# Attention plus mixture-of-experts on one core: another order of loads, copies and sums at the start of the attention part

## The chip, the cores and the metric

The kernel runs on one core of a Trainium2 chip. The metric is the device time of one execution in microseconds (us), lower is better. The core has five engines with their own instruction streams: TensorE (PE: matmuls and transposes; PEld: its weight loads), VectorE (DVE), ScalarE (ACT), GpSimd (POOL) and SyncE (SP), which here only issues transfers. Sixteen DMA engines move the data.

## The reference, cut to what matters

Four batches of eight heads, 768 tokens and 64 channels go through a local attention with block summaries, and the result goes through a top-1 mixture of eight experts. Per batch and head:

```python
block, window = 32, 16
k_sum = k.reshape(B, H, nb, block, D).max(axis=3)      # summary keys: maximum of 32 keys
v_sum = v.reshape(B, H, nb, block, D).mean(axis=3)     # summary values: mean of 32 values
scores_l = where(|i - j| < 16, scale * q @ k.T, -1e9)  # local part
scores_s = scale * q @ k_sum.T + log(block)            # 24 summaries
a = softmax(concat([scores_l, scores_s]))
attn = a @ concat([v, v_sum])
# x = attn as 3072 rows of 512; per row one expert e of 8:
out = gate * sigmoid(x @ w_output_gate)[e] * (relu(x @ w1[e]) @ w2[e])
```

The inputs q, k, v are 6.3 MB each in float32.

## The kernel before, in words

**Attention** works in 48 stages, `stages = [(b, tok, g)]`: batch `b` (4), tile of 128 tokens `tok` (6), half of the heads `g` (2). A pair of tiles is a step `u = tok // 2`; within a step the stages count `s = 0..3`. A stage `i` runs `scores(i)` (PE, line 338, into `sp`; then four masks with a minimum on DVE, line 346, and four exponentials on ACT, line 348), `turn_p(i)` (PE transposes, line 356, and an evacuation `pT` on ACT or DVE) and `values(i)` (PE, line 367, and the division on DVE, lines 375 to 377). In the loop `scores(i+1)` comes ahead of `turn_p(i)` and `values(i-1)`.

**Keys and queries** come in pieces of 256 tokens (`load`, line 209, 512 KB each, into `raw`). `reorder` (line 220 on DVE, 218 on ACT) copies a piece into `nat` so that two heads stand side by side. `prep_k` transposes it on PE (line 289, `ktr`), evacuates it into `kt` on ACT (line 201) and takes the maxima `km` on DVE (line 303); `k_sum` writes these into `kt` (line 312). `prep_q` does the same for queries (`qtr`, `qt`). The string `RE` says which engine reorders which piece: the first three are the key pieces of batch 0, then the query pieces 0 and 1 of batch 0, all later queries, all later keys.

**Values** are needed twice. `load_vw` (lines 271 and 272) loads for each block of 64 tokens a window of 64 + 32 rows into one of nine tiles `vw`. `load_vm` (line 228, 768 KB, four heads) loads the values for the means into `vm`; `v_sum` adds up 32 rows: on DVE for the first half of the heads of batch 0 (line 239), on POOL by halving additions for all others (lines 250 and 254). `mean` scales (line 260 or 262) and writes the 24 means of each head to the DRAM tensor `vs_dr` (line 263), and `load_vsum` (line 278) reads them back into each `vw` tile, behind the 64 + 32 rows. So a stage's `values` needs the means, by way of DRAM.

**What sets the order.** All loads of q, k, v, `vw`, means and weights are issued by SP, in the order of the program: a load whose source or buffer isn't ready holds up all loads behind it. The other engines' instructions are put in order ahead of time by a list scheduler that works with estimated durations and takes the program's order as priority; on the chip each engine then keeps that order. `tc.add_manual_dep(..., NoSync, SCHED_ONLY)` ties an instruction behind another in that order and adds no wait. Ahead of the attention, `route_setup` runs `WARM` = 44 matmuls of 128x128 bf16 on PE (line 161) whose result is not used, and POOL clears the nine `vw` tiles (line 191) and sets a column of ones in each (line 192).

The order of the program at the start is: key pieces 0, 1, 2, query piece 0, `vm` 0 and 1; reorder and prepare the keys, the queries; `k_sum`; `vw` of tile 0, query piece 1, `vw` of tile 1; the sums of values; reorder query piece 1; key piece 0 of batch 1; `vw` of tile 2; the means into tiles 0, 1, 2; `vm` 0 of batch 1; then the stages. In a stage with `g == 0` the loop reorders the next keys and queries ahead of `scores(i+1)`.

**The experts** start inside the last batch (`late_work`: lists, rows and weights of the first expert slot) and fill the time from about 190 us to the end, with PE in the lines 845 to 847 and 943 to 945.

Of the kernel before, what the change touches and what calls it, by code (L numbers as in the profile page):

```python
# [25 lines left out]
W = 120  # L26
# [8 lines left out]
VR = 9  # L35
VP = 72
ON_DVE = ("p1", "lt", "ls")
RE = "vavavvv"
SPLIT = 1
TAT = 0  # L40
XAT = 6
ROUTE_AT = (-1, 0, 1, 2, 4)
WARM = 44
SCALE = 1.0 / math.sqrt(D)
N, DM, E, F = B * S, H * D, 8, 1024
NT = N // P
# [131 lines left out]
def attention(tc, const, sa, sb, st, ps, dr, q, k, v, id_sb, c_sb, wg_sb, x_dr, l_dr, rt, late_work):  # L178
# [9 lines left out]
        KT.append(t)  # L188
    for i in range(VR):
        t = sb.tile([W, H, VP], F32, name=f"vw{i}", tag=f"vw{i}", bufs=1)  # L190
        nc.gpsimd.memset(t, 0.0)
        nc.gpsimd.memset(t[:, :, D:D + 1], 1.0)
        VW.append(t)
    def evac(what, dst, src, scale=None):
# [16 lines left out]
            src[b, :, 256 * u:256 * (u + 1), :].rearrange("h (p j) d -> p h (j d)", j=2))  # L211
        raws[kind, b, u] = raw

    def reorder(kind, b, u, engine="v"):
        t = (sa if kind == "k" else sb).tile([P, 2, H, D], F32, name=f"nat_{kind}{b}{u}", tag=f"nat{kind}", bufs=BUFS["nat" + kind])
        r = raws.pop((kind, b, u)).rearrange("p h j d -> p j h d")
        if engine == "a":
            nc.scalar.activation(t, r, AF.Copy)
        else:
            {"v": nc.vector, "p": nc.gpsimd}[engine].tensor_copy(t, r)  # L220
        nat[kind, b, u] = t

    vm = {}
# [9 lines left out]
    def v_sum(b, o, half):  # L233
        t = vm[b, o]
        if (b, o) == (0, 0):
            if half == 0:
                vs[b, o] = sb.tile([96, D], F32, name=f"vs{b}{o}", tag="vs", bufs=2)
            hs = slice(32 * half, 32 * half + 32)
            i = nc.vector.tensor_reduce(out=vs[b, o][:, hs], in_=t.rearrange("p (s d) -> p d s", d=D)[:, hs, :], axis=AX.X,
                                        op=ALU.add)  # L240

            tc.add_manual_dep(i.ins, km["last"].name, mybir.DependencyInfo(mybir.DependencyClass.NoSync,
                                                                           mybir.DependencyReason.SCHED_ONLY))
            if half == 1:
                mean(b, o, vs[b, o])
            return

        n = 16 * D
        if half == 0:
            nc.gpsimd.tensor_tensor(t[:, 0:n], t[:, 0:n], t[:, n:2 * n], ALU.add)  # L250
# [78 lines left out]
    def scores(i):  # L329
        b, tok, g = stages[i]  # L330
        u, tt = tok // 2, tok % 2
        qt, kt = QT[(3 * b + u) % 2], KT[b % 2]
        sp = ps.tile([P, 4, P], F32, name=f"sp{b}{tok}{g}", tag="S", bufs=PB["S"])
        for x in range(2):
            for y in range(2):
                li = 2 * tt + y
                blk = 4 * u + li
                nc.tensor.matmul(sp[:, 2 * x + y, 0:W], lhsT=qt[:, 2 * g + x, li, :],  # L338
                                 rhs=kt[:, 2 * g + x, blk * KW:blk * KW + W], start=True, stop=True)
        sm = sb.tile([P, 4, W], F32, name=f"sm{b}{tok}{g}", tag="sm", bufs=BUFS["sm"])  # L340
        mn = sb.tile([P, 4], F32, name=f"mn{b}{tok}{g}", tag="mn", bufs=BUFS["mn"])
        pr = sb.tile([P, 4, W], F32, name=f"pr{b}{tok}{g}", tag="pr", bufs=BUFS["pr"])
        for c in range(4):
            blk = 2 * tok + (c % 2)
            m = C_MASK + W * (1 if blk == 0 else (2 if blk == NB - 1 else 0))
            nc.vector.tensor_tensor_reduce(out=sm[:, c, :], in0=sp[:, c, 0:W], in1=c_sb[:, m:m + W], scale=1.0,  # L346
                                           scalar=3.0e38, op0=ALU.add, op1=ALU.min, accum_out=mn[:, c:c + 1])
# [173 lines left out]
    for i, (b, tok, g) in enumerate(stages):  # L521
# [31 lines left out]
        if b == B - 1:  # L553
# [1 line left out]
            take = w[:-(-len(w) // 2)] if g == 0 else w[:]  # L555
            del w[:len(take)]
            second += take
        if i + 1 < n:
            scores(i + 1)
        for work in first[:1]:  # L560
            work()
        turn_p(i)
        second = first[1:] + second
        for work in second:
            work()
        if i > 0:
            values(i - 1)
            pb, ptok, pg = stages[i - 1]
# [488 lines left out]
```

## Time and profile before

| what | value |
|---|---|
| time, median of 3 runs | 540.3 us (539.38 to 544.87) |
| profiled execution, own time | 537.39 us |
| its span in the trace | 535.6 us |
| PE busy | 492.9 us, 92% of the span |
| DVE / ACT / POOL busy | 387.0 / 336.2 / 204.1 us |
| granted TensorE clock, mean | 0.978 |
| moved by the DMA engines | 117.98 MB, mean 220 GB/s |

Times inside the profile count from the start of the span. A row of the timeline gives start, duration, engine, line, operation, output and input, how many instructions are merged in the row, and in brackets the idle time of the engine before it and what ended it. A row of the windows gives for a stretch of time the busy us of each engine with the number of instructions, the granted TensorE clock as a share of full speed (PEclk), the mean busy share of the DMA engines and what they moved. SPq rows are transfers being issued by SP, not the transfers.

### The profile page before, as it was taken

How to read it: one execution, taken by the hardware profiler on the slowest of the kernel's cores; microseconds unless marked ns; L12 is line 12 of the kernel's file. 1: busy time of each engine (PE TensorE's matmuls, PEld its weight loads, DVE VectorE, ACT ScalarE, POOL GpSimd, SP SyncE). 2: the span in 40 equal slices, each digit the busy share in tenths (PEclk: the TensorE clock that was granted, in tenths of full speed). 3: DMA queues.
4: the chain of work that ended last, by engine and by line, in shares of the span. 5: the costliest groups of instructions: out<-in, count | busy, mean ns of one | idle time of the engine just before them, and what ended most of it. 6: DMA issues, size and time to landing. Idle time of an engine off the chain costs nothing.

```text
span 535.6 us, 12274 instructions
## 1 busy us (share of the span) xinstructions
PE 492.9 (92%) x3880; PEld 428.5 (80%) x3880; DVE 387.0 (72%) x1238; ACT 336.2 (63%) x753; POOL 204.1 (38%) x231
## 2 busy tenths in 40 slices
PE   5899998789987999999999999999999999999990
PEld 5687887587766798789898998989897887987870
DVE  8877888479958868987666667675667767768660
ACT  4776786487769756554655656565567567558460
POOL 7527157245443432333735071421333421611321
PEclk9789999899999999999999999999999999999996
DMA  8989999899698577595966749486476796696640
GB/s 246 242 207 249 231 247 207 178 222 263 157 196 226 167 236 253 190 193 183 331 205 218 230 166 319 143 284 214 183 264 204 258 304 237 216 311 241 198 159 30
DMA packets 117052, 117.98 MB, mean 220 GB/s; under 512 B 53787, under 2 KB 78651, under 8 KB 116192
## 3 DMA queue, kind: packets, MB, share of 16 engines
q1 hardware_dynamic: 107584, 97.02, 64.5%
q0 software_dynamic: 9376, 19.91, 11.3%
q8 instruction: 36, 0.59, 0.5%
q14 instruction: 56, 0.46, 0.3%
HBM read 106.30 MB, written 13.79 MB: 224 GB/s over the span
## 4 chain that ended last, share of the span: by engine, by line
PE 61%; DMA 17%; DVE 6%; SPq 5%; issue 4%; ACT 3%; POOL 0%; POOLq 0%; ACTq 0%; DVEq 0%
PE hp L846 8%; PE hp L845 8%; PE hp L847 8%; PE yp L945 7%; PE yp L943 7%; PE yp L944 7%; DMA xg<-x_dr,lst_w 5%; PE sp L338 4%; DMA raw_q<-in_q_dram 4%; DMA vw<-vs_dr 3%; PE pv L367 3%; DMA raw_k<-in_k_dram 2%; PE pt L356 2%; PE xp L827 2%; SPq L272 1%
## 5 line engine op out<-in xcount | busy, mean ns | idle before, releaser
L845 PE MATMUL hp<-xhl,w1h 128*128 128x256 f32 x384 | 108.4, 284 | 1.1 <-ACT w2h L815 1.1
L846 PE MATMUL hp<-xhl,w1h 128*128 128x256 f32 x384 | 108.8, 284 | 0.0
L847 PE MATMUL hp<-xhl,w1l 128*128 128x256 f32 x384 | 108.5, 283 | 0.1
L943 PE MATMUL yp<-w2h,hh 128*128 128x512 f32 x216 | 86.5, 401 | 0.3 <-ACT hh L914 0.2
L945 PE MATMUL yp<-w2h,hl 128*128 128x512 f32 x216 | 84.9, 395 | 0.1
L944 PE MATMUL yp<-w2l,hh 128*128 128x512 f32 x216 | 84.9, 393 | 0.0
L794 POOL DMA_INDIRECT xg<-x_dr,lst_w x26 | 30.5, 1173 | 123.5 <-PE xp L827 118.7
L845 PEld LDWEIGHTS hp<-xhl,w1h 128*128 128x128 f32 x384 | 73.2, 191 | 2.9 <-issue 1.5
L846 PEld LDWEIGHTS hp<-xhl,w1h 128*128 128x128 f32 x384 | 73.5, 191 | 2.1 <-DVE xhl L830 0.9
L847 PEld LDWEIGHTS hp<-xhl,w1l 128*128 128x128 f32 x384 | 73.5, 191 | 0.3 <-issue 0.3
L348 ACT ACTIVATE pr<-sm,mn 128x120 f32<-128x120 f32 x192 | 61.5, 386 | 18.3 <-DVE mn L346 17.9
L848 ACT ACTIVATE hh<-hp 128x256 fp32r<-128x256 f32 x96 | 35.2, 380 | 53.4 <-PE hp L847 43.6
L849 DVE SCALAR_TENSOR_TENSOR hl<-hp,hh 128x256 fp32r<-128x256 f32 x96 | 38.8, 419 | 37.6 <-ACT hh L848 22.9
L338 PE MATMUL sp<-kt,qt 128*128 128x120 f32 x384 | 53.6, 287 | 2.2 <-DVE mn L346 0.8
L338 PEld LDWEIGHTS sp<-kt,qt 128*128 128x128 f32 x384 | 48.4, 199 | 5.6 <-issue 2.3
L945 PEld LDWEIGHTS yp<-w2h,hl 128*128 128x128 f32 x216 | 40.4, 188 | 9.8 <-DVE hl L915 1.2
L346 DVE CUSTOM_DVE_ANT_0 sm<-sp,c_sb 128x120 f32<-128x120 f32 x192 | 42.2, 276 | 8.2 <-PE sp L338 5.3
L943 PEld LDWEIGHTS yp<-w2h,hh 128*128 128x128 f32 x216 | 40.7, 188 | 8.6 <-ACT hh L914 0.7
L944 PEld LDWEIGHTS yp<-w2l,hh 128*128 128x128 f32 x216 | 40.7, 188 | 7.9
L356 PE MATMUL pt<-id_sb,pr 128*120 128x128 f32 x192 | 38.7, 288 | 4.6 <-ACT pr L348 1.9
L367 PE MATMUL pv<-vw,pT 120*64 120x65 f32 x768 | 36.3, 231 | 6.8 <-DVE xs L377 2.8
L367 PEld LDWEIGHTS pv<-vw,pT 120*64 120x64 f32 x768 | 28.6, 139 | 16.0 <-issue 7.9
(736 smaller groups left out, 1039.5 us busy)
## 6 DMA issues: line engine op xcount, KB each, us to landing
vw<-in_v_dram SPq DMA_DIRECT2D x88, 96.0 KB
raw_k<-in_k_dram SPq DMA_DIRECT2D x12, 512.0 KB
raw_q<-in_q_dram SPq DMA_DIRECT2D x12, 512.0 KB
vm<-in_v_dram SPq DMA_DIRECT2D x8, 768.0 KB
x_dr<-xs POOLq DMA_DIRECT2D x24, 256.0 KB
vw<-vs_dr SPq DMA_DIRECT2D x36, 48.0 KB
vw<-in_v_dram SPq DMA_DIRECT2D x8, 64.0 KB
xg<-x_dr,lst_w POOLq DMA_INDIRECT x26
```

The lines of the kernel that those rows point to most:

```text
L338: nc.tensor.matmul(sp[:, 2 * x + y, 0:W], lhsT=qt[:, 2 * g + x, li, :], rhs=kt[:, 2 * g + x, blk * KW:blk * KW + W], start=True, stop=True)
L346: nc.vector.tensor_tensor_reduce(out=sm[:, c, :], in0=sp[:, c, 0:W], in1=c_sb[:, m:m + W], scale=1.0, scalar=3.0e38, op0=ALU.add, op1=ALU. ...
L348: nc.scalar.activation(pr[:, c, :], sm[:, c, :], AF.Exp, bias=mn[:, c:c + 1], scale=-1.0)
L356: nc.tensor.transpose(pt[:, c, :], pr[:, c, :], id_sb)
L367: nc.tensor.matmul(po[64 * y:64 * y + 64, 2 * x + hh, :], lhsT=pT[:, 2 * x + y, 64 * hh:64 * hh + 64], rhs=VW[(NB * b + 2 * tok + y) % VR] ...
L845: nc.tensor.matmul(hp, lhsT=w_h[:, fs], rhs=self.xh[:, c, :], start=c == 0, stop=False)
L846: nc.tensor.matmul(hp, lhsT=w_h[:, fs], rhs=self.xl[:, c, :], start=False, stop=False)
L847: nc.tensor.matmul(hp, lhsT=w_l[:, fs], rhs=self.xh[:, c, :], start=False, stop=c == NC - 1)
L849: nc.vector.scalar_tensor_tensor(hl[:, j, :], hp, 0.0, hh[:, j, :].bitcast(F32), ALU.max, ALU.subtract)
L943: nc.tensor.matmul(y, lhsT=hh[:, j, tk], rhs=w_h, start=j == 0, stop=False)
L944: nc.tensor.matmul(y, lhsT=hh[:, j, tk], rhs=w_l, start=False, stop=False)
L945: nc.tensor.matmul(y, lhsT=hl[:, j, tk], rhs=w_h, start=False, stop=j == NF - 1)
```

## The change

The loads of `vm` for batch 0 are moved ahead of the keys, its sums stand ahead of the key preparation in the program and no longer behind `k_sum`, and the means are read back for tiles 0 and 1 ahead of key piece 0 of batch 1 and `vw` of tile 2. The first three key pieces and query piece 0 are all reordered by ACT (pieces 0 and 2 of the keys were DVE's). Query piece 1 of batch 0 is reordered behind the masks of stage 1; the later reorders of queries, and of the key pieces 1 and 2 of the next batch, move from the stages with `g == 0` to the end of the step's last stage (`s == 3`), tied behind the masks of `scores(i+1)` or behind `k_sum`. The key piece 0 of the next batch is tied behind `k_sum` of the current one. `WARM` goes from 44 to 130. Eight of the nine `vw` tiles are no longer cleared, and of the first only 32 partitions.

```diff
-RE = "vavavvv"
+RE = "aaaavvv"
-WARM = 44
+WARM = 130
...
         t = sb.tile([W, H, VP], F32, name=f"vw{i}", tag=f"vw{i}", bufs=1)
-        nc.gpsimd.memset(t, 0.0)
+        if i == 0:
+            nc.gpsimd.memset(t[0:32], 0.0)
         nc.gpsimd.memset(t[:, :, D:D + 1], 1.0)
...
-    def reorder(kind, b, u, engine="v"):
+    def reorder(kind, b, u, engine="v", after=None):
...
-            {"v": nc.vector, "p": nc.gpsimd}[engine].tensor_copy(t, r)
+            i = {"v": nc.vector, "p": nc.gpsimd}[engine].tensor_copy(t, r)
+            if after is not None:
+                tc.add_manual_dep(i.ins, after.name, ... NoSync, SCHED_ONLY)
...
             # v_sum, first half of the heads of batch 0
-            i = nc.vector.tensor_reduce(out=vs[b, o][:, hs], ...)
-            tc.add_manual_dep(i.ins, km["last"].name, ... NoSync, SCHED_ONLY)
+            nc.vector.tensor_reduce(out=vs[b, o][:, hs], ...)
...
     # scores(i) now returns its last mask instruction
-            nc.vector.tensor_tensor_reduce(out=sm[:, c, :], ...)
+            mask = nc.vector.tensor_tensor_reduce(out=sm[:, c, :], ...)
+        return mask.ins
...
+    load_vm(0, 0, 1)
     for u in range(3):
         load("k", k, 0, u)
     load("q", q, 0, 0)
-    load_vm(0, 0, 1)
+    for o in range(2):
+        for half in range(2):
+            v_sum(0, o, half)
     for u in range(3):
         reorder("k", 0, u, RE[u])
         prep_k(0, u)
...
     load_vw(0, 0)
     load("q", q, 0, 1)
     load_vw(0, 1)
-    for o in range(2):
-        for half in range(2):
-            v_sum(0, o, half)
+    for tok in range(2):
+        load_vsum(0, tok)
...
-    reorder("q", 0, 1, RE[4])
     load_ahead(1, -2)
     load_vw(0, 2)
-    for tok in range(3):
-        load_vsum(0, tok)
+    load_vsum(0, 2)
     load_ahead(1, -1)
...
         # in the loop over the stages
             if n2 and tt == 0:
                 load("q", q, *n2)
-            elif n2:
-                reorder("q", *n2, RE[5])
             load_ahead(*((b + 1, tok) if tok < 4 else (b + 2, tok - 6)))
-            if more and tok in (0, 1, 3):
-                reorder("k", b + 1, (tok + 1) // 2, RE[6])
+            if more and tok == 0:
+                reorder("k", b + 1, 0, RE[6], km["last"])
...
-        if i + 1 < n:
-            scores(i + 1)
+        mask = scores(i + 1) if i + 1 < n else None
+        if i == 0:
+            reorder("q", 0, 1, RE[4], mask)
         for work in first[:1]:
             work()
         turn_p(i)
         second = first[1:] + second
         for work in second:
             work()
+        if s == 3 and more and u < 2:
+            reorder("k", b + 1, u + 1, RE[6], mask)
+        if s == 3 and n2:
+            reorder("q", *n2, RE[5], km["last"] if u == 2 else mask)
         if i > 0:
             values(i - 1)
```

More of the change, by code (lines that the diff above doesn't have):

```diff
@@ L219, in reorder @@
         else:
-            {"v": nc.vector, "p": nc.gpsimd}[engine].tensor_copy(t, r)
+            i = {"v": nc.vector, "p": nc.gpsimd}[engine].tensor_copy(t, r)
+            if after is not None:
+                tc.add_manual_dep(i.ins, after.name, mybir.DependencyInfo(mybir.DependencyClass.NoSync,
+                                                                          mybir.DependencyReason.SCHED_ONLY))
         nat[kind, b, u] = t
@@ L238, in v_sum @@
             hs = slice(32 * half, 32 * half + 32)
[L239 to L243, printed above, removed]
+            nc.vector.tensor_reduce(out=vs[b, o][:, hs], in_=t.rearrange("p (s d) -> p d s", d=D)[:, hs, :], axis=AX.X,
+                                    op=ALU.add)
             if half == 1:
@@ L345, in scores @@
             m = C_MASK + W * (1 if blk == 0 else (2 if blk == NB - 1 else 0))
-            nc.vector.tensor_tensor_reduce(out=sm[:, c, :], in0=sp[:, c, 0:W], in1=c_sb[:, m:m + W], scale=1.0,
-                                           scalar=3.0e38, op0=ALU.add, op1=ALU.min, accum_out=mn[:, c:c + 1])
+            mask = nc.vector.tensor_tensor_reduce(out=sm[:, c, :], in0=sp[:, c, 0:W], in1=c_sb[:, m:m + W], scale=1.0,
+                                                  scalar=3.0e38, op0=ALU.add, op1=ALU.min, accum_out=mn[:, c:c + 1])
             nc.scalar.activation(pr[:, c, :], sm[:, c, :], AF.Exp, bias=mn[:, c:c + 1], scale=-1.0)
         prs[i] = pr
+        return mask.ins
     def turn_p(i):
```

## The prediction

> **What bounds the kernel now.** I read the windows of ten microseconds first, to see which engine is full where, with the clock beside it.
>
> ```profile
> span 535.6 us, 12274 instructions
> ...
> 0.00:10.00 10.00, 6.38 (x58) 6.12 (x59) 7.83 (x12) 3.15 (x6) 8.87 (x25) 1.00 0.83 251
> 10.00:20.00 10.00, 7.22 (x37) 6.13 (x34) 9.97 (x18) 6.34 (x17) 2.48 (x12) 0.67 1.10 250
> 20.00:30.00 10.00, 8.61 (x54) 7.30 (x53) 6.25 (x41) 8.12 (x24) 5.35 (x8) 0.84 0.81 166
> 30.00:40.00 10.00, 9.94 (x122) 8.36 (x122) 7.95 (x41) 7.97 (x23) 3.79 (x3) 0.97 1.01 259
> 50.00:60.00 10.00, 10.00 (x125) 8.41 (x126) 9.54 (x56) 8.45 (x23) 2.49 (x5) 1.00 1.09 239
> ```
>
> After the length come the busy us of PE, PEld, DVE, ACT and POOL, then the clock, the DMA share and GB/s. From 30 us on PE is busy 97 to 100% and the DMA engines are full too. Before that PE does little: the clock is 0.67 and 0.84 of full, and in 20 to 30 the DMA engines drop to 0.81. So the start is a time of late work, and what follows moves with it. The later part is PE:
>
> ```profile
> 100.00:150.00 50.00, 44.22 (x496) 36.45 (x496) 41.37 (x224) 33.24 (x90) 23.52 (x27) 0.97 0.94 207
> 150.00:200.00 50.00, 44.05 (x494) 37.80 (x495) 37.46 (x190) 37.19 (x93) 19.15 (x22) 1.00 0.78 211
> 250.00:300.00 50.00, 50.00 (x332) 45.72 (x331) 32.34 (x59) 27.94 (x58) 25.80 (x24) 1.00 0.69 233
> ```
>
> The experts (from about 200) have a full PE and gain nothing themselves: a gain ahead of them arrives at the end whole, one in DMA alone does not. Between 100 and 200 PE stands for nearly 12 us.
>
> Second view: the timeline of SP, POOL and DVE at the start, for what makes the hole at 26 us.
>
> ```profile
> 24.07 0.53 SPq L272 DMA_DIRECT2D vw<-in_v_dram  x1
> 27.99 2.48 SPq L278 DMA_DIRECT2D vw<-vs_dr  x6
> ...
> 18.42 2.36 POOL L250 TENSOR_TENSOR vm<-vm 96x1024 f32<-96x1024 f32 x1 [7.52 <-DMA vm<-in_v_dram]
> 25.42 0.57 POOL L263 DMA_DIRECT2D vs_dr<-vm  x1 [0.30 <-POOL vm L262]
> ...
> 15.95 3.70 DVE L239 TENSOR_REDUCE vs<-vm 96x32 f32<-96x1024 f32 x2
> 19.57 0.27 DVE L346 CUSTOM_DVE_ANT_0 sm<-sp,c_sb 128x120 f32<-128x120 f32 x1
> 19.77 0.27 DVE L346 CUSTOM_DVE_ANT_0 sm<-sp,c_sb 128x120 f32<-128x120 f32 x1
> 28.37 0.28 DVE L346 CUSTOM_DVE_ANT_0 sm<-sp,c_sb 128x120 f32<-128x120 f32 x1 [0.99 <-PE sp L338]
> 33.24 0.27 DVE L346 CUSTOM_DVE_ANT_0 sm<-sp,c_sb 128x120 f32<-128x120 f32 x1
> ...
> 26.00:28.00 2.00, 1.41 (x9) 1.40 (x9) 0.69 (x1) 1.55 (x3) 0.00 (x0) 0.78 0.18 35
> 28.00:30.00 2.00, 2.00 (x12) 1.95 (x10) 0.90 (x8) 1.07 (x4) 0.00 (x0) 0.50 0.26 59
> ```
>
> SP ends an issue at 24.60 and starts the next at 27.99: it waits for the means in DRAM, which POOL writes at 25.42. For 3.4 us no load is issued, and the DMA engines run empty (0.18, 0.26). The rows of line 346 are my stage clock: first mask 19.57 (behind the sums of values, which hold DVE to 19.65), stage 4 at 28.37, stage 5 at 33.24.
>
> **The change, part by part.**
>
> *Loads of `vm` first.* The rows for the price:
>
> ```profile
> 6.09 2.35 DVE L220 COPY nat_k<-raw_k 128x1024 f32<-128x1024 f32 x1
> 7.61 1.06 ACT L218 ACTIVATE nat_k<-raw_k 128x1024 f32<-128x1024 f32 x1 [5.58 <-DMA raw_k<-in_k_dram]
> 9.19 2.32 ACT L201 ACTIVATE kt<-ktr 128x256 f32<-128x256 f32 x8 [0.51 <-PE ktr L289]
> 12.20 0.66 ACT L201 ACTIVATE kt<-ktr 128x256 f32<-128x256 f32 x2 [0.69 <-PE ktr L289]
> 15.00 2.41 ACT L201 ACTIVATE qt<-qtr 64x512 f32<-64x512 f32 x4 [0.66 <-PE qtr L289]
> ```
>
> Key pieces 0 and 1 of 512 KB were taken up at 6.09 and 7.61, 1.52 us apart. Two `vm` of 768 KB ahead of them cost by that 2 x 2.28 = 4.6 us: keys at about 10.7, 12.2 and 13.7, the query at 15.2.
>
> *All four reorders on ACT.* ACT then has 4 x 1.06, the key evacuations 2.32 + 0.66 + 0.66 (two rows of two) and the query's 2.41: 10.3 us. From 10.7 that is 21.0, with two waits for PE of the size shown (0.51, 0.66) 22.2. The scores started 1.3 us after the query's evacuations began (16.30 against 15.00, row below), so at 22.2 - 2.4 + 1.3 = 21.1, and the first mask about 0.6 us on at full clock: **21.7 against 19.57, 2.1 us later**. DVE's copies (2.35 for the first) vanish, but DVE wasn't late there; this part buys nothing by itself.
>
> *Sums ahead of the keys.* The sums leave the stretch ahead of the first mask: before they held it to 19.65, though the scores had begun at 16.30; that gain is inside the 21.7 already. POOL's chain took from 18.42 to 25.99. With its `vm` landing ahead of the first key, near 9, it ends near 16.5, and the means are in DRAM before SP gets to line 278 (which it reaches no sooner than 20, since the loads ahead are the same bytes). So **SP's wait of 3.4 us goes**. The four read-backs that now stand ahead of key piece 0 and `vw` of tile 2 cost 4 x 0.41 us of issue (2.48 for six), which is only a change of order.
>
> *Warm-ups.*
>
> ```profile
> 1.07 4.87 PE L161 MATMUL warm<-ones 128*128 128x128 bf16 x44 [1.07 <-DVE ones L157]
> 8.49 1.97 PE L289 MATMUL ktr<-id_sb,nat_k 128*128 128x128 f32 x16 [2.56 <-DVE nat_k L220]
> 13.85 1.97 PE L289 MATMUL qtr<-id_sb,nat_q 128*128 128x128 f32 x8 [1.26 <-ACT nat_q L218]
> 16.30 3.74 PE L338 MATMUL sp<-kt,qt 128*128 128x120 f32 x16 [0.48 <-issue]
> ```
>
> 44 take 4.87 us, 0.111 each, and no full-speed row of that shape exists. Bounds: all 130 at 0.111 end at 1.07 + 14.4 = 15.5 us; if the 86 further ones run twice as fast (transposes took 0.123 each at 8.49 and 0.246 at 13.85, in the ten us with the mean clock of 0.67) they end at 5.94 + 4.8 = 10.7. I take 10.7 to 12, since the transposes at 8.49 were already fast; then PE is free when the keys come. At 15.5 they'd be in the way: rival C. The Trainium skill, in "TensorE: Matmul & The Clock Gate", Part 1, says the PE starts at half rate and is let go after some 3.4 us of steady work, with 56 ns for this shape then; an estimate from that page ends the 130 near 10 us. This trace shows no such step within its 4.87 us, so it doesn't settle it. The same page has the clock halved again after about one idle window of 3.4 us; that speaks against this edit, because ACT's chain leaves PE mostly idle from 11 to 21. By the trace the mean clock of 10 to 20 us was 0.67 though PE counted as busy for 7.22 of the ten: I count on a drop for the first scores, as before, and take no gain for the warm-ups there.
>
> *`vw` not cleared.* POOL's 9 x 0.6 us (5.4 us in all) go. They lay beside loads and slowed DVE's first copies; with these on ACT the gain is nothing that lasts.
>
> *Sum of the start.* First mask 21.7; eight masks, one each 0.2 us (19.57, 19.77), are done at 23.3; query piece 1 is copied by 24.1 (its load, taken up at 21.95 before, keeps its place in bytes). Before, the copy ended at 23.12 and stage 4's mask came 5.25 us later, 0.85 of it at half clock: 28.5, level with 28.37. From there to stage 5 were 4.87 us, of which the clock of 0.50 up to 30 cost half of 1.6 us, 0.8: stage 5 at 32.6, **0.6 ahead**. The DMA side is 3.4 ahead. Both PE and DMA are full after that, so the gain lies between, and `values` of the first stages, which waited for the means, fill PE's holes earlier: I take **-2.0 us**, bounds -3.4 and, if the later keys win over everything, +2.1.
>
> *Copies that stand back.* DVE waits for raw queries in order, with masks and divisions behind it:
>
> ```profile
> 48.25 1.19 DVE L220 COPY nat_q<-raw_q 128x1024 f32<-128x1024 f32 x1 [3.42 <-DMA raw_q<-in_q_dram]
> 100.53 0.69 DVE L220 COPY nat_q<-raw_q 128x1024 f32<-128x1024 f32 x1 [3.61 <-DMA raw_q<-in_q_dram]
> 154.99 0.69 DVE L220 COPY nat_q<-raw_q 128x1024 f32<-128x1024 f32 x1 [2.73 <-DMA raw_q<-in_q_dram]
> ...
> 102.28 1.14 PE L367 MATMUL pv<-vw,pT 120*64 120x65 f32 x16 [2.80 <-DVE xs L377]
> 155.84 0.66 PE L387 MATMUL xtr<-id_sb,xs 128*128 128x128 f32 x4 [1.28 <-DVE lg L197]
> ...
> L338 PE MATMUL sp<-kt,qt x384: 268/275/537, 16.3 to 185.4; 128*128 128x120 f32 x192
> ...
> 45.42 0.42 PE L367 MATMUL pv<-vw,pT 120*64 120x65 f32 x4 [1.08 <-DMA vw<-vs_dr]
> ...
> 145.00 9.97 DMA raw_q<-in_q_dram
> ```
>
> The scores of the 48 stages begin from 16.3 to 185.4, 3.6 us each. The copy moves back by one stage and four masks (0.8), some 4.4 us, more than each of these waits. So the two PE stalls that follow a copy, 2.80 and 1.28, may go; less a copy (0.69) that still stands ahead of the next transposes: **-3.4 us**. The wait at 48.25 I put at nothing: PE's stall there (45.42) was ended by a read-back. What is late next is `prep_q` and `prep_k`, which now follow their copy in the very next stage; the bounds are 0 (they stall PE instead) and -5.7 (both stalls and the half clock after the first, rows 102 to 106 at 0.56 and 0.59, 1.6 us).
>
> ```profile
> 102.00:104.00 2.00, 1.72 (x24) 1.15 (x24) 0.89 (x3) 0.00 (x0) 1.18 (x2) 0.56 0.50 84
> 104.00:106.00 2.00, 2.00 (x13) 1.46 (x10) 1.71 (x8) 0.49 (x2) 1.53 (x2) 0.59 0.72 173
> ```
>
> *Sum:* -2.0 - 3.4 = -5.4 on the profiled 537.4: 532.0. The median shown is 2.9 above that execution, so 534.9; I write **535.0**.
>
> **The rivals.**
>
> *A, hidden anyway (0.23).* The loads keep the same bytes and the stalls follow the loads, not the copies: PE then waits in `qtr` for what DVE waited for. For it: the raw query of 145.00 took 9.97 us to land, so the transfer itself is long. Start -1 and copies 0: 537 to 541, taken at 539.5.
>
> *B, both in full (0.19).* Start -3.4, copies -5.7, and the read-back stall at 45.42 with it (1.08): -10, so 530. For it: DMA and PE are both full right behind the hole, and a shift there is carried on.
>
> *C, slower (0.10).* The warm-ups never speed up and hold PE to 15.5, which no row excludes. ACT then has two reorders and all evacuations left, 2.1 + 6.05 us, from 16.0, plus 0.66: 24.8; scores at 23.7, first mask at 24.6, 5.0 later than now. With nothing from the copies and the half clock in the first scores 546. It decides from a first mask later than about 24: beyond that, the hole at 26 us is no longer what is late.
>
> *D, not what it says.* The list scheduler may place the tied copies where they were. That is a part of A.
>
> **How the numbers follow.** The forecast (535.0, own range 531.5 to 538.5) has 0.48, A 0.23, B 0.19, C 0.10. About 1% (5.4 us) is what a measurement of this kernel can tell from no change; the bound lies at 534.9. B and half of the forecast's case are below it: 0.43. The other half and A are within: 0.47. C is slower: 0.10. The range of eight in ten goes from 528.5 (the lower part of B is left out) to 542.5 (all of A; C is left out).
>
> **What would show it.** Right: no wait of SP ahead of line 278 and a DMA share near 1 in 26 to 30; first mask between 21 and 22.5; stage 5 before 33; warm-ups ending near 11; no PE stall over 1.5 us behind a copy of a query. Wrong: a first mask past 24, PE waiting in line 289 for `nat_q` as long as DVE did, or a mean clock of 10 to 30 us below the 0.67 and 0.84 of before. The weakest step is the second: 3.4 us from two stalls of one execution, whose places move when the start moves.

## The result, and the profile after

The changed kernel takes 548.4 us (median of 18 runs, 543.9 to 551.3) against 541.9 us for the kernel before (18 runs beside it, 536.6 to 551.4): a ratio of **1.0134, 95% interval 1.0106 to 1.0162**. It is slower by 1.3%, some 7.3 us by the ratio. The forecast was 535.0, and its range ended at 542.5. The profiled execution took 546.23 us, its span 544.0. The ratios here and below leave out executions more than 1.5% above the fastest of their kernel, such as one of e11's four, at 1194 us, and the one of e13 that was profiled.

The windows of the changed kernel, in the columns of the prediction (busy us of PE, PEld, DVE, ACT and POOL, then clock, DMA share and GB/s):

```profile
0.00:10.00 10.00, 8.94 (x127) 8.94 (x127) 6.55 (x10) 1.28 (x1) 5.13 (x26) 1.00 0.80 195
10.00:20.00 10.00, 4.40 (x29) 3.99 (x27) 2.73 (x6) 5.19 (x11) 6.58 (x8) 0.83 1.08 279
20.00:30.00 10.00, 7.93 (x77) 7.02 (x75) 8.21 (x43) 9.55 (x27) 0.00 (x0) 1.00 0.85 188
26.00:28.00 2.00, 2.00 (x21) 2.00 (x20) 2.00 (x16) 1.98 (x7) 0.00 (x0) 1.00 0.47 120
28.00:30.00 2.00, 2.00 (x30) 1.72 (x28) 1.91 (x14) 2.00 (x8) 0.00 (x0) 1.00 1.22 311
150.00:200.00 50.00, 40.38 (x440) 35.27 (x440) 34.50 (x175) 33.29 (x86) 17.54 (x21) 0.90 0.66 170
```

Two stretches differ. From 10 to 20 us PE works 4.40 us (7.22 before), although the clock is better. From 150 to 200 it works 40.38 us (44.05 before) at a clock of 0.90 (1.00 before). The hole in the DMA at 26 us, by contrast, is half filled: share 0.47 where it was 0.18, and 1.22 behind it (0.26).

The timeline of the start (lines stand a little lower than before: L220 is the ACT copy of L218, L245 the sum of L239, L253 the addition of L250, L281 the read-back of L278, L292 the transposes of L289, L349 the masks of L346):

```profile
1.06 9.32 PE L161 MATMUL warm<-ones 128*128 128x128 bf16 x130 [1.06 <-DVE ones L157]
7.33 3.72 DVE L245 TENSOR_REDUCE vs<-vm 96x32 f32<-96x1024 f32 x2 [1.86 <-DMA vm<-in_v_dram]
12.21 2.33 POOL L253 TENSOR_TENSOR vm<-vm 96x1024 f32<-96x1024 f32 x1 [5.96 <-DMA vm<-in_v_dram]
14.62 1.06 ACT L220 ACTIVATE nat_k<-raw_k 128x1024 f32<-128x1024 f32 x1 [3.28 <-DMA raw_k<-in_k_dram]
15.73 3.40 PE L292 MATMUL ktr<-id_sb,nat_k 128*128 128x128 f32 x16 [5.34 <-ACT nat_k L220]
18.84 0.59 POOL L266 DMA_DIRECT2D vs_dr<-vm  x1 [0.30 <-POOL vm L265]
23.86 1.61 SPq L281 DMA_DIRECT2D vw<-vs_dr  x4
24.76 0.28 DVE L349 CUSTOM_DVE_ANT_0 sm<-sp,c_sb 128x120 f32<-128x120 f32 x1 [0.65 <-PE sp L341]
33.47 0.27 DVE L349 CUSTOM_DVE_ANT_0 sm<-sp,c_sb 128x120 f32<-128x120 f32 x1
```

The first key is taken up at 14.62, where it was 6.09, because two loads of values come ahead of it. The first mask is at 24.76 (before 19.57), stage 4 at 33.47 (before 28.37). The start is 5.2 us late.

Most of that lateness is made up on the way. I use the time at which POOL starts to write the output of a tile (L384, before L380) as a milestone. Tile (0,5), the last of batch 0, is 4.7 us later than before (67.85 against 63.17); tile (1,4) is 0.65 us *earlier*, (2,5) 1.2 us earlier. Each is read from one execution; e5 below, which has the order of before, has its tiles up to 2.2 us and its end 3.5 us later than before, so smaller differences say little.

```profile
101.87 0.58 POOL L384 DMA_DIRECT2D x_dr<-xs  x1 [2.23 <-DVE den L379]
149.09 0.58 POOL L384 DMA_DIRECT2D x_dr<-xs  x1
175.61 0.60 POOL L384 DMA_DIRECT2D x_dr<-xs  x1 [10.50 <-DVE xs L381]
```

against, in the kernel before,

```profile
102.52 0.58 POOL L380 DMA_DIRECT2D x_dr<-xs  x1 [8.04 <-DVE xs L377]
150.30 0.58 POOL L380 DMA_DIRECT2D x_dr<-xs  x1 [1.66 <-DVE mn L346]
171.53 0.61 POOL L380 DMA_DIRECT2D x_dr<-xs  x1 [4.43 <-DVE xs L377]
```

Tile (3,0) is 4.1 us late again, and the first output of the experts is 5.3 us late (227.41 against 222.10). So some 5 us are lost between 149 and 176 us. The span ends 8.4 us later (544.0 against 535.6); the other 3.1 us are lost behind the first output, among the experts. The timeline of ACT and PE from 151 us:

```profile
151.26 0.40 ACT L351 ACTIVATE pr<-sm,mn 128x120 f32<-128x120 f32 x1
158.51 0.63 ACT L823 ACTIVATE w1h<-raw_('e', 0)_0_2671 128x512 fp32r<-128x512 f32 x1 [6.84 <-DMA raw_('e', 0)_0_2671<-in_moe_w_dram]
159.78 0.58 ACT L203 ACTIVATE pT<-pt 120x512 f32<-120x512 f32 x1
160.41 1.20 PE L371 MATMUL pv<-vw,pT 120*64 120x65 f32 x16 [5.83 <-ACT pT L203]
160.00:164.00 4.00, 3.59 (x27) 3.47 (x28) 3.33 (x23) 3.94 (x10) 2.03 (x2) 0.50 1.09 247
```

ACT's next instruction is the copy of an expert's first weight (L823), whose load has not landed. Behind it in ACT's order stands `pT` of a tile that PE had finished by 153.3. PE waits 5.83 us and then runs at half clock. In the kernel before, the same copy stands behind `pT` and `qt`, and waits for nothing:

```profile
154.60 0.60 ACT L201 ACTIVATE pT<-pt 120x512 f32<-120x512 f32 x1 [0.79 <-PE pt L356]
157.88 1.19 ACT L201 ACTIVATE qt<-qtr 64x512 f32<-64x512 f32 x2
159.97 0.61 ACT L815 ACTIVATE w1h<-raw_('e', 0)_0_2593 128x512 fp32r<-128x512 f32 x1
```

No line of the change touches that copy. The order in which the engines' instructions are written comes from a list scheduler, and an edit anywhere can redraw it: in a line by line comparison of the first 3,000 instructions of each engine, with the numbers of the tiles left out, 24% of PE's, 16% of DVE's and 7.5% of ACT's stand in another place than before. The shares further down are counted in the same way. That order is the theory the experiments had to weigh against the late start.

### The profile page after: what moved, and what is told of

Its sections match the earlier page's. It is cut to its first block, busy times and chain, and to the rows that moved or that the text cites. A ratio compares the mean times of both kernels' runs of the same rounds, so it can differ in the third digit from the quotient of the medians.

```text
span 544.0 us, 12435 instructions
## 1 busy us (share of the span) xinstructions
PE 498.7 (92%) x3966; PEld 435.5 (80%) x3966; DVE 387.4 (71%) x1236; ACT 338.4 (62%) x755; POOL 201.2 (37%) x223
## 4 chain that ended last, share of the span: by engine, by line
PE 43%; DMA 7%; issue 3%; DVE 2%; ACT 1%; POOL 0%; SPq 0%; POOLq 0%; ACTq 0%; DVEq 0%
PE hp L854 7%; PE hp L853 7%; PE hp L855 7%; PE yp L953 7%; PE yp L952 7%; PE yp L951 7%; DMA xg<-x_dr,lst_w 5%; PE xp L835 2%; DMA raw_('w', 7)_0_6237<-in_moe_w_dram 1%; DMA raw_('w', 9)_7_6674<-in_moe_w_dram 1%; DVE w2l L824 1%; ACT w1h L823 0%; POOL out_dram L976 0%; DVE y L973 0%; ACT w2h L823 0%
## 5 line engine op out<-in xcount | busy, mean ns | idle before, releaser
L341 PE MATMUL sp<-kt,qt 128*128 128x120 f32 x384 | 54.7, 291 | 1.8 <-ACT qt L203 1.1
L341 PEld LDWEIGHTS sp<-kt,qt 128*128 128x128 f32 x384 | 50.4, 205 | 4.2 <-issue 1.7
L349 DVE CUSTOM_DVE_ANT_0 sm<-sp,c_sb 128x120 f32<-128x120 f32 x192 | 42.8, 277 | 10.4 <-PE sp L341 8.0
L953 PEld LDWEIGHTS yp<-w2h,hl 128*128 128x128 f32 x216 | 40.4, 188 | 10.1 <-DVE hl L923 1.6
L371 PE MATMUL pv<-vw,pT 120*64 120x65 f32 x768 | 38.2, 232 | 6.0 <-ACT pT L203 5.8
```

Source lines behind the costliest of these rows:

```text
L349: mask = nc.vector.tensor_tensor_reduce(out=sm[:, c, :], in0=sp[:, c, 0:W], in1=c_sb[:, m:m + W], scale=1.0, scalar=3.0e38, op0=ALU.add, o ...
L371: nc.tensor.matmul(po[64 * y:64 * y + 64, 2 * x + hh, :], lhsT=pT[:, 2 * x + y, 64 * hh:64 * hh + 64], rhs=VW[(NB * b + 2 * tok + y) % VR] ...
L953: nc.tensor.matmul(y, lhsT=hl[:, j, tk], rhs=w_h, start=False, stop=j == NF - 1)
```

## The experiments

Each kernel was run beside the kernel before; "first mask" and the tiles are read from the trace as above, in us; the end is that of the span.

| kernel | ratio, interval | first mask | (1,4) | (2,5) | first output | end |
|---|---|---|---|---|---|---|
| before | 1 | 19.57 | 102.52 | 150.30 | 222.10 | 535.6 |
| changed | 1.0134, 1.0106–1.0162 | 24.76 | 101.87 | 149.09 | 227.41 | 544.0 |
| e5 72 warm-ups, same order | 0.9983, 0.9933–1.0033 | 19.55 | 103.84 | 150.83 | 223.91 | 539.1 |
| e8 80 warm-ups, new order | 1.0075, 1.0028–1.0121 | 20.07 | 100.30 | 151.49 | 222.72 | 541.9 |
| e11 90 warm-ups, new order | 1.0117, 1.0040–1.0193 | 20.11 | 98.28 | 151.56 | 230.86 | 546.7 |
| e7 values first | 1.0071, 1.0026–1.0117 | 28.57 | 106.84 | 157.17 | 228.37 | 545.3 |
| e12 late read-backs | 1.0006, 0.9970–1.0042 | 19.71 | 99.48 | 152.92 | 222.74 | 538.2 |
| e4 new start alone | 1.0174, 1.0117–1.0230 | 24.32 | 102.44 | 163.09 | 225.48 | 543.2 |
| e15 copies alone | 1.0075, 1.0043–1.0106 | 19.72 | 96.96 | 150.76 | 224.68 | 538.9 |
| e17 copies, early queries | 1.0272, 1.0184–1.0359 | 19.56 | 104.53 | 154.62 | 233.39 | 548.7 |

### The parts of the change

**e4, the new start without the copies that stand back**, and **e15, those copies alone**:

```
 e4, against the changed kernel (shortened):
+    reorder("q", 0, 1, RE[4])              # at the start again
...
+            elif n2:
+                reorder("q", *n2, RE[5])
-            if more and tok == 0:
-                reorder("k", b + 1, 0, RE[6], km["last"])
+            if more and tok in (0, 1, 3):
+                reorder("k", b + 1, (tok + 1) // 2, RE[6])
...          # and without the reorders behind scores(i+1) and at s == 3
 e15: the kernel before, with the same places changed the other way round
```

> The changed kernel with the reorders where they were before (all of the start's edits stay: loads of vm first, sums ahead, ScalarE reorders, 130 warm-ups, no clearing). Its ScalarE order in the last batch has the weight copy ahead of pT, as in the changed kernel. Theory 1: late start +5, nothing made up, stall +5: 551 to 552, first mask near 24.8 as in the changed kernel. Theory 2: 547 to 549, as the changed kernel, the moved copies being worth nothing.

> The kernel before with only the copies of later pieces standing back (as in e3, but with the weight copies left where the scheduler puts them). Theory (the copies' gain is hidden by the loads, and a redrawn order costs): first mask 19.6, the waits for raw queries gone up to tile (1,4), 3 to 5 us ahead there, nothing left at tile (2,5), time 1.0 to 1.012. Forecast of the prediction (the gain arrives): 0.99 to 0.996. Rival (the tie spoiled it in e3): 0.995 to 1.003.

Both are slower than before, by 1.7% (9.4 us) and 0.75% (4.1 us), and the intervals exclude the gains of the prediction. Together they cost 7.3, so they aren't terms that add up. e4's first mask is 4.8 us late, yet its tile (0,5) stands at 62.53, level with 63.17: the late start is made up within batch 0. (Its late (2,5) is made up at the next tile, 172.83 against 171.53.) In e15 tile (1,4) is 5.6 us ahead. That need not be the copies: e11 and e12, whose copies stand where they did, are 4.2 and 3.0 ahead there.

```profile
96.96 0.58 POOL L385 DMA_DIRECT2D x_dr<-xs  x1 [1.19 <-DVE xs L382]
```

Then DVE comes to the next copy of a query before its load has landed, and the lead is gone:

```profile
115.30 0.69 DVE L221 COPY nat_q<-raw_q 128x1024 f32<-128x1024 f32 x1 [3.92 <-DMA raw_q<-in_q_dram]
116.64 1.14 PE L372 MATMUL pv<-vw,pT 120*64 120x65 f32 x16 [4.33 <-DVE pT L198]
```

The kernel before took up the same query at 117.07, after a wait of 1.01 us: the load came 1.8 us sooner, too little to keep the lead. At (2,5) e15 is 0.5 us behind. From 145 us on it has the stall behind the weight as well (ACT waits 5.1 us, PE 3.4).

**e1**, the changed kernel with the weight copies of the first expert tied behind the stage's last exponential, and **e3**, the copies alone with the same tie (shortened):

```
-            nc.scalar.activation(hi, raw, AF.Copy)
+            cp = nc.scalar.activation(hi, raw, AF.Copy)
+            tc.add_manual_dep(cp.ins, rt["last_exp"].name, SCHED_ONLY)
```

> The changed kernel, with one edit: in the last batch, ScalarE's copies of the first expert's weights (w1h, w2h) are tied behind the last exponential that is emitted before them, so that they can't stand ahead of a stage's pT and qt evacuations in ScalarE's order; no wait is added or taken away. Theory 1 (a third of the loss is ScalarE standing 6.8 us behind a weight load at 151.5 us): PE's idle 5.83 us at 154.6 goes, time 5 us below the changed kernel, some 543. Theory 2 (the late keys alone cost the 7 us; the weights are late anyway and the stall only shows it): no change from the changed kernel, 547 to 549.

> The kernel before with only the moved reorders (query piece 1 behind the masks of stage 1, later queries and keys at the end of a step's last stage) and the weight copies tied as in the other run; the start is that of before. Theory 1: the moved copies take away VectorE's waits for raw queries at 48, 100 and 155 us; the changed kernel made up some 6 us between tile 1 of batch 0 and tile 4 of batch 1: 5 us faster, 536. Theory 2 (that catching up was only the slack of loads that were late anyway, and a kernel that isn't late has none to make up): within 1.5 us of before, 541 to 543.

e1 ran at 1.0113 (1.0059 to 1.0168), e3 at 1.0114 (1.0068 to 1.0161); in e3 PE waited 4.2 us for DVE's work on the tied weights instead. In e1 the stall behind the weight is gone (the longest wait of PE from 150 to 175 us is 2.2) and the first output stands at 223.22, 1.1 us behind before in place of 5.3. But its end is 9.5 us late (545.1). Of that 3.3 us are lost between the sixth and the seventh output (272.42 to 296.30, in before 270.05 to 290.64), where PE works 8.41 of ten us:

```profile
270.00:280.00 10.00, 8.41 (x60) 7.15 (x60) 2.31 (x5) 2.72 (x7) 4.80 (x5) 1.00 0.16 58
```

The interval of e1 includes the time of the changed kernel. So the stall behind the weight is where the changed kernel's trace loses most of its time, but **taking it away did not bring the time back**; I can't call it the cause.

### The start

**e7**, before with its two loads of values ahead of the keys and nothing else; **e6**, the changed kernel with keys first again and the sums behind `k_sum`:

```
 e7:
+    load_vm(0, 0, 1)
     for u in range(3):
         load("k", k, 0, u)
     load("q", q, 0, 0)
-    load_vm(0, 0, 1)
 e6: the reverse in the changed kernel, with the sums where before has them
```

> The kernel before with one edit: the two vm loads stand ahead of the keys. Keys come some 5 to 8 us later, as in the changed kernel. Theory S: first mask 24 to 25, time +5 to +7, 546 to 548. Theory O says the same for the time (its order differs from before's too), so the test is the course: by S the tiles are late by the same 4 to 6 us from the first to the last; by O the offset comes and goes between batches and the last batch adds its own stall.

> The whole change except the loads: keys and query piece 0 come first again, vm behind them, and the sums of values stand behind k_sum again. Theory S (the late start carries through: first mask 24.8 against 19.6): the first mask is back near 21 and the time falls by 5, to 541 to 543. Theory O (the list scheduler's order of the whole attention was drawn anew and is worse than before's, wherever the start is): first mask near 21 as well, but 546 to 549, as the changed kernel.

e7's first mask is 9.0 us late, and its time 0.7% (3.8 us) up. e6, which was to mend the start, ran at 1.0246 (1.0156 to 1.0335), its first mask at 28.29: with the sums back in DVE's way, PE waited 4.9 us for DVE's key copies. A late start is not carried on one to one: by e7 some four tenths of it (3.8 of 9.0), and that includes whatever its redrawn order (17% of PE's instructions) costs.

**e12** moves only the read-backs of means behind a load that doesn't need them:

```
-    for tok in range(3):
-        load_vsum(0, tok)
     load_ahead(1, -1)
+    for tok in range(3):
+        load_vsum(0, tok)
```

> The kernel before with one edit: the six read-backs of means stand behind the load of the next batch's first vm in SP's order, so SP issues that load at 24.6 in place of waiting 3.4 us; nothing else is moved by hand, but the scheduler redraws the order (19% of PE's rows). Start theory (the hole at 26 us is worth something): DMA share in 26 to 28 rises from 0.18 to over 0.6, milestones of tile (0,5) 1 to 3 us earlier than 63.2; time 0.995 to 1.0. Theory of the redrawn order: the same hole is filled, and yet 1.003 to 1.012. Rival (hidden): 1.0 within 0.003.

```profile
26.00:28.00 2.00, 1.40 (x11) 1.16 (x12) 0.00 (x0) 1.94 (x4) 0.44 (x1) 1.00 1.08 184
25.92 0.83 SPq L228 DMA_DIRECT2D vm<-in_v_dram  x1
29.63 2.48 SPq L278 DMA_DIRECT2D vw<-vs_dr  x6
```

SP issues the load at 25.92 and waits for the means afterwards, from 26.75 to 29.63. The hole that the prediction valued at up to 3.4 us is full (share 1.08 in place of 0.18), and the time is the same: 1.0006 (0.9970 to 1.0042). It is the only edit of the kernel before with a new order that cost nothing; whether filling the hole paid for that order, this run can't say.

### The warm-ups and the order

**e5**, **e8** and **e11** are the kernel before with one number changed:

```
-WARM = 44
+WARM = 72     # e5; 80 in e8, 90 in e11
```

> The kernel before with WARM = 72. By the instruction lists every engine's order is that of before; only 28 warm-ups are added in a stretch in which PE stood idle (5.94 to 8.49 us). Both theories: no change, 539 to 543, unless the warm-ups themselves buy clock: then the mean clock of 10 to 20 us rises from 0.67 and the time falls by up to 3 us. It is the measure for what a run without any change of order can differ.

> The kernel before with WARM = 80: the warm-ups end near 7.8 us, while PE had nothing to do before 8.49, so nothing is late by itself; but the list scheduler's estimate now has PE busy when the keys come, and it draws another order (a fifth of PE's rows stand elsewhere). Theory S: time follows the first mask; if that is within 1 us of 19.6, then 540 to 543. Theory O: 545 to 550 although nothing but the order changed.

> The kernel before with 90 warm-ups: by the row of the changed kernel (130 end at 10.38, fast ones 0.056 each) they end near 8.1, before the first transposes at 8.49, so nothing of PE's work is moved by them in time; the scheduler's order is redrawn (21% of PE's rows, 10% of DVE's). A second draw beside that with 80 (1.0075). Theory (the order of before is a good draw, others cost): 1.004 to 1.012, first mask 19.5 to 20.3. Rival (80 was an accident): 0.998 to 1.003.

With 72 and 80 the warm-ups end before PE's first transposes, which start where they did (8.49 and 8.48); with 90 they reach up to them, and the transposes start at 8.64. The rows of e8 and e11:

```profile
1.07 5.99 PE L161 MATMUL warm<-ones 128*128 128x128 bf16 x80 [1.07 <-DVE ones L157]
8.48 1.75 PE L289 MATMUL ktr<-id_sb,nat_k 128*128 128x128 f32 x14 [1.42 <-DVE nat_k L220]
```

```profile
1.06 7.74 PE L161 MATMUL warm<-ones 128*128 128x128 bf16 x90 [1.06 <-DVE ones L157]
8.64 1.59 PE L289 MATMUL ktr<-id_sb,nat_k 128*128 128x128 f32 x13
```

With 72 the engines keep the order of before (ACT and DVE to the last row), and the time is the same. With 80 and 90 the scheduler writes another order (PE 20 and 21%, DVE 12 and 10%), and the time goes up by 0.75% and 1.2%. Beside the added warm-ups, which PE does while it has nothing else to do (but for 0.15 us in e11), nothing differs: **a redrawn order alone cost 4.1 and 6.3 us**, beside the changed kernel's 7.3. The place differs from that in the changed kernel. In e8's trace the first output is 0.6 us late and the end 6.3, so nearly all is lost among the experts. In e11 the last batch stalls behind a query:

```profile
158.42 0.69 DVE L220 COPY nat_q<-raw_q 128x1024 f32<-128x1024 f32 x1 [7.17 <-DMA raw_q<-in_q_dram]
159.86 0.47 PE L356 MATMUL pt<-id_sb,pr 128*120 128x128 f32 x1 [7.47 <-ACT pr L348]
```

**e2** has all 130 on the kernel before; **e9** and **e10** are the changed kernel with 170 and 44:

```
-WARM = 44
+WARM = 130    # e2, on before
-WARM = 130
+WARM = 170    # e9, on the changed kernel; 44 in e10
```

> The kernel before with WARM = 130 in place of 44 and nothing else. PE has idle time at 6 to 8.5 us, and 130 warm-ups ended at 10.4 us in the changed kernel, so the first key transposes move from 8.5 to 10.4. Theory 1: the start costs 0 to 2 us, but the list scheduler's order of ScalarE in the last batch flips as in the changed kernel (weight copy ahead of pT), so the stall of 5 to 6 us behind the weight load is there too: +5, some 547. Theory 2: within 2 us of the kernel before, 541 to 543.

> The changed kernel with 170 warm-ups in place of 130. At 0.056 us each the 40 more end at about 12.6, and PE's first transposes there began at about 15, so PE's real work is not later; but the instruction order written by the scheduler is redrawn (10% of PE's rows, 6% of DVE's stand elsewhere). First mask 24.8 in every theory. Theory (a redrawn order costs or gains by itself): the time differs from the changed kernel's 1.013 by 0.4% or more, most likely it lies between 1.005 and 1.02. Rival (the time follows from the start): 1.013 within 0.003, the same milestones.

> The changed kernel with 44 warm-ups as before. The keys come at 14.6, so the 130 warm-ups (end 10.4) can't be late; they could only help the clock. Theory (warm-ups are neutral where PE waits for keys, what differs is the redrawn order): first mask 24.5 to 25.5, time 1.005 to 1.02. Rival (warm-ups help the clock of the first transposes): the transposes and first scores run at half rate, first mask 1 to 2 us later, time 1.015 or more. Rival (86 more warm-ups cost clock afterwards): mean clock up by 0.003 or more and time under 1.008.

e2 ran at 1.0261 (1.0207 to 1.0315), with its first mask at 27.13: the sums of values are again ahead of it on DVE, and the key copies ahead of those are slow (last section). e9 gave 1.0127 (1.0057 to 1.0198), the time of the changed kernel, with 10% of PE's order redrawn; so this redraw did not move the time. e10 gave 1.0197 (1.0135 to 1.0259) although its first mask was 1.0 us earlier (23.72). In both, ACT stands ahead of `pT` in front of the weight's load (waits of 5.8 and 5.0 us) as in the changed kernel.

### Are the loads what holds the tiles?

In most kernels tile (2,5) stood at 149 to 153, and before and the changed kernel moved 222 and 224 GB/s in their first 150 us. **e13** (before) and **e14** (changed) leave out 39 loads of value rows, so that a part of their result is other data:

```
-            nc.sync.dma_start(t[LW + NS:LW + NS + n, ...], v[b, ...])
+            if NB * b + blk < VR:
+                nc.sync.dma_start(t[LW + NS:LW + NS + n, ...], v[b, ...])
```

> The kernel before without the second of the two loads of each block of value rows in batches 1 to 3 (96 KB each, 39 of them, 3.7 MB in all, some 2.9 MB of it ahead of 150 us; those blocks keep the rows of an older block, so that part of the result is other data). Theory (the loads' bytes set the pace of batches 1 to 3): 2.9 MB at 222 GB/s are 13 us; tile (2,5) comes 6 to 13 us earlier than 150.3, the waits for raw queries vanish, time 0.975 to 0.99. Rival (the order of the engines' instructions sets it, loads are hidden): tile (2,5) within 2 us, time 0.998 to 1.01, as with other redrawn orders.

> The changed kernel without the same loads (the second load of each block of value rows in batches 1 to 3, other data in that part of the result). Theory (bytes set the pace): tile (2,5) 6 to 13 us earlier than 149.1, and the 6.8 us wait of ScalarE for the first expert weight in the last batch shrinks to under 2 us since the weights come earlier; time 0.985 to 1.0, that is lower by 1.3% or more than the changed kernel's 1.013. Rival (late start and order): tile (2,5) within 2 us and time 1.005 to 1.02; the stall behind the weight stays.

That theory fell. The order is redrawn here too, but the 13 us that it promised would show beside that. With fewer loads the time was 1.0095 (1.0042 to 1.0147) and 1.0162 (1.0022 to 1.0302), and tile (2,5) came 6 and 8 us *later*. The waits of SP from 60 to 160 us in e13 and e14, and of DVE from 24 to 160 us in e13, say why less traffic didn't bring the queries sooner:

```profile
SPq L271 <- PE pv L368: 21.0, 7, 6.6
...
SPq L274 <- PE pv L372: 25.2, 8, 7.3
...
DVE nat_q L220 <- DMA raw_q<-in_q_dram: 12.0, 6, 3.8
```

SP stands 21.0 us in e13 (2.2 in before) and 25.2 in e14 (3.8 in the changed kernel) until PE's `values` free a block of the ring of value rows, and the query's load is issued behind that. The loads run only as far ahead as PE's progress lets them.

**e16** (before), **e17** (copies alone) and **e18** (changed) issue the query's loads one tile earlier:

```
-            if n2 and tt == 0:
+            n3 = step_after(b, u, 3)       # one piece further on
+            if (b, tok) == (0, 0):
                 load("q", q, *n2)
...
+            if n3 and tt == 1:
+                load("q", q, *n3)
```

> The kernel before with the loads of raw queries issued one tile earlier in SP's order (ahead of that tile's loads of value rows), the copies where they were. Theory (late issue): VectorE's waits for raw queries between 24 and 160 us shrink from 13 us to under 4, tile (2,5) 2 to 6 us ahead of 150.3, time 0.988 to 0.998. Rival (a redrawn order costs whatever is moved, and stalls appear elsewhere): waits shrink, but tile (2,5) within 2 us and time 1.0 to 1.012.

> The copies alone that stand back (as in e15), with the query loads issued one tile earlier. Theory (late issue took the gain back): the waits for raw queries (8.3 us in e15) go, PE's stall of 4.3 us behind a copy at 116 us goes, tile (2,5) 4 to 8 us ahead of 150.8, time 0.985 to 0.998. Rival (redrawn order): stalls appear elsewhere, time 1.003 to 1.012.

> The changed kernel with the query loads issued one tile earlier. Its waits for raw queries were 1.9 us only, so the theory of late issue expects little here by tile (2,5) (0 to 2 us), and a stall of ScalarE behind the first expert weight as before or longer (5 to 8 us); time 1.008 to 1.015. Rival (the queries' loads are what is late in the changed kernel too): time under 1.005.

They ran at 1.0120 (1.0050 to 1.0191), 1.0272 (1.0184 to 1.0359) and 1.0228 (1.0127 to 1.0329). e17 lies furthest from what was expected. The longest waits of its DVE from 24 to 160 us hold no query any more (e15 had 8.3 us of them, before 12.3):

```profile
DVE sm L350 <- PE sp L342: 6.9, 8, 1.4
...
DVE nat_k L221 <- DMA raw_k<-in_k_dram: 5.3, 6, 1.2
```

The wait that this edit was made for is gone (that for keys grew from 1.7 to 5.3 us), and the kernel is 2.7% slower than before. No kernel of this study beats the one before.

## Why the prediction was wrong

The forecast added up -2.0 us for the start and -3.4 for the copies. Run by themselves they came to +9.4 (e4) and +4.1 (e15), each with a redrawn order in it. Both terms failed, the second in its mechanism.

**The start: the loads put first were mis-sized.** The two loads of values ahead of the keys were priced at 4.6 us by the pace of two keys; the first key came 8.5 us later (14.62 against 6.09). The loads' own landings show it: DVE took up the first at 7.33 and POOL the second at 12.21, 4.9 us apart and not 2.28. The DMA engines were full, and yet they moved less than while the kernel before loaded its keys (the changed kernel from 2 to 12 us, then before from 4 to 10):

```profile
2.00:12.00 10.00, 8.38 (x123) 8.21 (x121) 7.02 (x11) 0.28 (x2) 4.24 (x22) 1.00 1.01 239
4.00:10.00 6.00, 3.44 (x33) 3.18 (x31) 5.42 (x10) 1.87 (x5) 6.00 (x11) 1.00 1.16 358
```

At 239 GB/s the 1.57 MB take 6.6 us; what else shared the engines I did not separate. In the prediction's own fence the rows of 251 and 250 GB/s would have given 6.3. e7, which moves these loads alone, has its first mask 9.0 us late. The next step, ACT's chain, held: first key to first mask was forecast at 11.0 us and took 10.1.

**SP's wait stayed.** The means were to be in DRAM by 16.5, since their values would land near 9. They landed near 12, POOL issued the write at 18.84, and SP, which was ready at 21.5, waited 2.3 us until 23.86. This is the same mis-sized load, one step on. In e12 the hole is filled and no time is won, so the 3.4 us that were allowed for it did not show.

**The warm-ups were right**, at 10.38 where 10.7 to 12 was taken: the first 38 take until 5.1 us, 0.106 each, the other 92 take 5.3 us, 0.058 each. The Trainium skill ("TensorE: Matmul & The Clock Gate", Part 1), by whose step the estimate was near 10, is borne out, though the step came 4.0 us after the first warm-up here, 2.9 in e10 and 6.0 in e2. After 5.34 us of idle the first 16 transposes took 3.40 us, where they took 1.97 before, and the granted clock was 0.50 from 16 to 18 us; the page's rule that an idle window halves the clock again is borne out too. Rival C's warm-ups did not happen, though its point of decision (a first mask later than 24) and a time near its price (546) came about by the mis-sized loads; that agreement is luck, since by the milestones the late start was made up before (1,4).

**The copies that stand back did not take the waits away.** In the changed kernel DVE's waits for raw queries from 24 to 150 us fell from 9.5 us to 1.9, as forecast. But in e15, where only the copies move, they are 8.3, and in e4, where the copies stay where they were, 2.4 (in this order: before, changed, e15, e4):

```profile
DVE nat_q L220 <- DMA raw_q<-in_q_dram: 9.5, 5, 3.6
DVE nat_q L222 <- DMA raw_q<-in_q_dram: 1.9, 1, 1.9
DVE nat_q L221 <- DMA raw_q<-in_q_dram: 8.3, 3, 4.0
DVE nat_q L222 <- DMA raw_q<-in_q_dram: 2.4, 3, 1.3
```

In e8, with 36 more warm-ups and nothing else, they are 3.5. So the fall came with the new start or the new order and not with the copies, and the -3.4 us had no such mechanism behind them.

**The sum took gains to be carried on.** It let gains made at the start, at 102 and at 156 us arrive at the end, because PE and DMA were full behind them. The prediction's own rows had PE idle for nearly 12 us between 100 and 200, and e15's lead of 5.6 us at (1,4) was gone at (2,5): the engines wait for each other and for loads in a fixed order, and one that comes early waits there. Nor do the experts take the same time whatever comes ahead of them. From the first output to the end were 313.5 us in before and 314.2 to 321.9 in the other 19 traces. Rival A, which had the gain of the copies hidden, comes nearest in this part.

**A term was missing.** No step priced what any edit does to the order that the scheduler writes for the other 12,000 instructions. e8 and e11 measured it: 0.75% and 1.2% with next to nothing else changed. In the changed kernel it put a weight's copy ahead of `pT`, and ACT waited 6.84 us in front of it. The Trainium skill ("PSUM — Partial Sum Buffer", Engine vs sequencer instructions) calls ScalarE's queue a strict FIFO; the row shows it, `pT` at 159.78 right behind the weights.

Of the signs named in the prediction, "first mask past 24" came true on the side of wrong; "a mean clock of 10 to 30 us below the 0.67 and 0.84" did not (0.83 and 1.00), so the clock of the start was not the loss.

**What stays open.** How the 7.3 us divide between the late start and the redrawn order isn't settled: every edit that changes one redraws the other. Redraws alone gave 4.1 and 6.3 us; e9's moved nothing against the changed kernel. What the experts lose, 3.1 us in the changed kernel's trace and 5.7 in e8's, has no cause shown. All 17 other kernels with a new order, whatever their edit, measured between 1.0006 and 1.0272, none below 1, so the order of before looks a favourable one; why, no single stall explains, since e1 and e17 each removed a named stall and gained nothing. A run with the order of before held fast under the new start, which would divide the two, wasn't tried. Leaving the blocks of `vw` uncleared and giving ACT all four reorders weren't tried by themselves either.

## What to carry to other kernels

Price a load that is put first by landings of its own kind, not by the distance between landings of another (here 4.9 us and not 2.28). Where a scheduler writes the order, first measure a control that changes no work but makes it write anew: here it moved the time by 0.75 to 1.2%, more than each term of the sum. Before a wait's end is put down to an edit, run the edit alone: here the wait fell in kernels without the edit and stayed in the one that had only it. And follow a milestone to the end of the span before adding up a gain in the middle.

## What the runs showed of the hardware

DVE's small key copies took 0.30 us each in before, with POOL idle (the three in this row overlap by their ends), and up to 2.04 in e2, where they fell beside POOL's additions:

```profile
15.29 0.74 DVE L312 COPY kt<-km 128x288 f32<-128x288 f32 x3
```

```profile
19.25 2.04 DVE L312 COPY kt<-km 128x288 f32<-128x288 f32 x1
21.21 0.30 DVE L312 COPY kt<-km 128x288 f32<-128x288 f32 x1
21.43 1.37 DVE L312 COPY kt<-km 128x288 f32<-128x288 f32 x1
18.78 2.34 POOL L250 TENSOR_TENSOR vm<-vm 96x1024 f32<-96x1024 f32 x1 [7.90 <-DMA vm<-in_v_dram]
21.20 1.43 POOL L254 TENSOR_TENSOR vm<-vm 96x512 f32<-96x512 f32 x1
```

The first copy begins while POOL adds and ends at 21.29, 0.17 us after that addition (21.12); the third ends at 22.80, 0.17 after the next (22.63). The copy between them, begun 0.01 us after that next addition, takes its 0.30. So two copies that met a running addition lasted until it was over, and one that began together with an addition did not. e6 has a case of the first kind: a copy from 21.55 to 23.02, an addition of POOL from 20.52 to 22.86.

That is part of why e2, in which only the number of warm-ups and with it the order differs, had its first mask 7.6 us late: work that is harmless in one order is slow in another, beside another engine's.
